# A reciprocal as a power on GpSimd, a second bank, a swapped decoding step and new ranks in an attention and mixture kernel

## The chip, the cores and the metric

One core of a Trainium2 chip. The metric is the device time of one execution, in microseconds (us). The kernel before ran three times: 2363.28, 2365.78 and 2366.66 us; the median is 2365.78 us.

## The reference

Three layers follow one another, on 4 x 576 = 2304 tokens of width 512 (8 heads of 64):

```python
scores = scale * np.matmul(q, k.transpose(0, 1, 3, 2))
kth = np.partition(scores, -top_k, axis=-1)[..., -top_k:-top_k + 1]      # top_k = 32
scores = np.where(scores >= kth, scores, -1000000000.0)
attn = np.exp(scores - np.max(scores, axis=-1, keepdims=True))
attn = attn / (np.sum(attn, axis=-1, keepdims=True) + 1e-09)
x = np.matmul(attn, v)                        # heads side by side: 2304 x 512
...
h = x @ w_in                                  # 512 -> 2048
x = (h * np.cos(h)) @ w_out                   # 2048 -> 512
...
P = np.exp(logits - logits.max())             # logits = x @ w_gate, 8 experts
for _ in range(8):
    P /= P.sum(1, keepdims=True) + 1e-09
    P /= P.sum(0, keepdims=True) + 1e-09
    P *= N / E
for e in range(E):
    out += P[:, e:e + 1] * (np.maximum(x @ w1[e], 0.0) @ w2[e])
```

`w_in` and `w_out` reach the kernel as 64-bit numbers, which it turns into 32-bit ones itself.

## The kernel before, in words

**How the work is cut.** The first three tiles of 128 tokens (the leading tiles) go through attention and the first MLP ahead of everything else, in plain 32-bit matmuls (`attention_tile`, `moe1_tile_a`, `moe1_tile_b`). Their output (`x2fh`, `x2fl`) lets the expert matmuls of these tiles begin (`fill`), which then run on TensorE beside the attention of the rest (`attention`, `moe1`). Later matmuls split every operand into a high and a low part and take three products (lines 506 to 508; 517, 518 and 521 where the low part comes late). After the rest of the attention come the remaining tiles of the first MLP, the gates, and the experts for all other tokens.

**The leading stage.** For each of the 24 (tile, head) pairs `att_tile` multiplies queries and keys (line 582), copies the scores (588), and finds the 32 largest of each row on VectorE in four rounds (590, 593, 594). GpSimd computes the offset of the exponential (595), ScalarE does a leaky step and the exponential with its sum (596, 597). GpSimd adds 1e-9 to the sum (599), VectorE takes the reciprocal (600), GpSimd multiplies the row by it (601). TensorE transposes the row (606), ScalarE copies it (610), TensorE multiplies by the values (664), ScalarE copies the result (668). The attention of the other tokens goes through the same lines, 120 times more, with 624, 625, 632 and 634 in place of 610 and 664.

Beside it the weights are decoded, 16 blocks of `w_in` and 16 of `w_out`, each 128 x 512 (`decode`, called by `fresh` and `pieces`). A DMA brings the block, VectorE shifts the high word (461), ScalarE scales the low word (462), GpSimd adds 768 to the high word (463) and ScalarE takes the sign of what is above 768 (464); GpSimd adds the shifted word and the low word as integers (465) and multiplies by the sign (466). A second DMA keeps the result for the later MLP.

The first MLP of a leading tile: products with `w_in` (762) into two banks in turn, copies (764), the factor cos(h) in `gate` (724 to 731, on GpSimd, VectorE, ScalarE, VectorE), transposes in groups of four (772) into the banks of `trb` in turn, copies (775), 16 second products with `w_out` accumulated in one bank (785), a copy (787), transposes (792), and the two parts of the output (799, 800).

**What sets the order.** Nothing is issued as it stands in the code. `Plan.add` keeps each instruction with its engine, a cost in ns and what it depends on; `Plan.listed` plays the engines forward in time, and gives each engine, whenever it is free, the ready instruction of lowest priority value. The value is that of the class of work (`PRIORITY`); in the leading stage a number from `ORDER` is added, one for each engine, kind of work and unit (a pair of tile and head, a half of a tile's MLP or its second product, a block). The order so found is the order in which each engine then runs, fixed before the launch. `Plan.settle` goes through it once more with paces (`PACE`, or 1.15 times the cost) and puts filler matmuls (line 1203, into a bank of their own) into TensorE's expected gaps, up to 230 us.

The lines that the change touches or that the steps of the prediction name:

```python
hb, trb = Cycle([ps_y[0], ps_h]), Cycle([ps_y[2], ps_y[1]])     # line 748
...
y = ps_y[3]                                                     # line 783
```

So two transposed groups may stand in two banks, and the second products of all three tiles use the same bank.

Of the kernel before, what the change touches and what calls it, by code (L numbers as in the profile page):

```python
# [10 lines left out]
F32 = mybir.dt.float32  # L11
# [3 lines left out]
AF = mybir.ActivationFunctionType  # L15
ALU = mybir.AluOpType
# [6 lines left out]
HALF_PI = 1.5707963267948966  # L23
# [22 lines left out]

ORDER = {
    ("PE", "first attention"): [
        -4.1, -3.9, -2.2, -3.2, -4.2, -2.1, -3.6, -2.9, -3, -3.3, -2.9, -2.6, -2.4, -3.9, -2.9, -2.9,
        -1.9, -2.9, -4.3, -2.9, -3.2, -1.8, -2.1, -3,  # L50
    ],
    ("PE", "first mlp"): [
        -0.8, -1.8, -1.6, 0, -1.1, -1.1, -0.9, 0, -1.5, -1.2, -1.8, 0,
    ],
    ("PE", "decode"): [
        0.7, 1.2, 1.8, 0.4, -0.8, -0.4, -0.4, -0.3, -1.5, -0.4, -0.1, -0.9, -2.1, 0.2, -1.5, -1.6,
        -0.8, -2.6, -0.3, 0.8, -1.5, -0.4, 0.2, -0.4, -0.4, -0.4, 0.3, 1.9, -0.7, -0.6, -0.4, -0.4,
# [12 lines left out]
    ("DVE", "first attention"): [  # L70
        -1, 0.2, -0.3, 0.2, -0.9, 0.8, -0.1, -0.7, 0.2, -0.2, -0.6, 0.6, 0.3, -1.7, 0.3, 0.7,
        0.7, 1, 1.1, 0.4, 0.2, 1.9, 0.2, -1.6,
    ],
    ("DVE", "first mlp"): [
        0.2, 1.2, 0.6, 0, -0.2, 0.8, 0.4, 0, -0.2, 1.1, -0.9, 0,
    ],
    ("DVE", "decode"): [
        -1.8, -0.6, -1.9, 0, -0.5, -2.3, 0.4, 0, -0.9, -0.3, -1.2, -1.1, -1.4, -0.3, -0.3, -1.2,
        -0.3, -2.5, 0, -0.6, -0.2, -0.3, -1.2, -0.1, -0.8, -0.3, 0.7, 0.3, 0, -0.3, -0.3, -2.2,
    ],  # L80
    ("POOL", "first attention"): [
# [58 lines left out]
class Plan:  # L140
# [15 lines left out]
    def buf(self, pool, shape, dtype, name):  # L156
        return Buf(self, pool, shape, dtype, name)
# [200 lines left out]
def fused_kernel(tc, kq, vv, w_in, w_out, w_gate, w1, w2, out, B=4):  # L358
# [4 lines left out]
    V, A_, G_, T_ = nc.vector, nc.scalar, nc.gpsimd, nc.tensor  # L363
# [23 lines left out]
    add, buf = pl.add, pl.buf  # L387
# [25 lines left out]
    x_d = buf("dram", [128, 4, NT], F32, "x_d")
    lg_d = buf("dram", [16, NT], F32, "lg_d")
# [5 lines left out]
    ps_y = [buf("psum", [128, 512], F32, f"y{i}") for i in range(4)]  # L420
    ps_h = buf("psum", [128, 512], F32, "h")
# [145 lines left out]
    def att_tile(stats, dests, plain=None):  # L567
# [4 lines left out]
        sc, m, wk, ex = sc_r(), m_r(), wk_r(), ex_r()  # L572
# [16 lines left out]
        mc = lambda i, k=1: m.ap[:, i : i + k]  # L589
# [7 lines left out]
        put("ACT", act_ns(S, ap=True) + 93.0, lambda: A_.activation(ex.ap, ex.ap, AF.Exp, scale=-0.125 / TINY, bias=mc(32), accum_out=mc(33)),  # L597
            [ex, (m, 32, 33)], [ex, (m, 33, 34)], func="exp")
        put("POOL", 162, lambda: G_.tensor_scalar(mc(34), mc(33), 1e-9, 1.0, op0=ALU.add, op1=ALU.mult), [(m, 33, 34)], [(m, 34, 35)])
        put("DVE", 75, lambda: V.reciprocal(mc(35), mc(34)), [(m, 34, 35)], [(m, 35, 36)])  # L600
        put("POOL", 724, lambda: G_.tensor_scalar(ex.ap, ex.ap, mc(35), 0.0, op0=ALU.mult, op1=ALU.add), [ex, (m, 35, 36)], [ex])  # L601
        pt = lambda: ps_t.ap.rearrange("p (c t) -> p c t", c=4)
        for c0, c1, p in ((0, 4, 128), (4, 5, 64)):
# [8 lines left out]
            for r0, rn, hd, t0 in dests:  # L612
# [629 lines left out]
```

## Time and profile before

| what | value |
|---|---|
| median of three runs | 2365.78 us |
| the profiled execution's own time | 2365.81 us |
| its span, first to last instruction | 2364.0 us |
| busy: TensorE (PE) | 2331.9 us, 99% |
| busy: weight loads (PEld) | 1932.1 us, 82% |
| busy: VectorE (DVE) | 1815.7 us, 77% |
| busy: ScalarE (ACT) | 1333.3 us, 56% |
| busy: GpSimd (POOL) | 1260.4 us, 53% |
| granted TensorE clock, mean | 0.998 of full |

The span is the time from the first instruction to the last; the execution's own time has 1.8 us more around it. The busy shares are averages over stretches with different limits, and matmuls are pipelined, with ends that are modelled: a busy PE is not a PE at its peak. In a row of the trace, "x" gives the count, "a<-b" the tile written and the tiles read, and "<-" in the last column what ended the idle time of the engine just before.

### The profile page before, as it was taken

The numbers are of one execution on the slowest core, as the hardware profiler recorded it, in microseconds if no ns is written. First come the engines' busy times: TensorE is split into PE (matmuls) and PEld (weight loads), VectorE is DVE, ScalarE is ACT, GpSimd is POOL, SyncE is SP. The second block draws the span as 40 slices with busy tenths as digits, with TensorE's granted clock in tenths as the row PEclk, the third lists the DMA queues.
The fourth block names the chain that finished last, engine by engine and source line by source line (L and its number), as shares of the span: only waits on it lengthen the run. The fifth ranks groups of instructions, "written<-read, shape, count | busy, mean of one in ns | idle before, by whom it ended". The sixth has DMA issues, their size and how long they took to land.

```text
span 2364.0 us, 34301 instructions
## 1 busy us (share of the span) xinstructions
PE 2331.9 (99%) x11487; PEld 1932.1 (82%) x11487; DVE 1815.7 (77%) x3340; ACT 1333.3 (56%) x2688; POOL 1260.4 (53%) x1352
## 2 busy tenths in 40 slices
PE   9999999999899999999999999999999999999999
PEld 7655989898677888888888897888888888888887
DVE  7991999999869999999177796876666666666665
ACT  5884888888787777777477675222232222222221
POOL 6982987888876666665401036433333344444440
PEclk9999999999999999999999999999999999999999
DMA  7661654555333333433443332122222221111101
GB/s 222 204 182 40 188 163 141 171 158 169 118 86 94 120 120 120 120 100 95 126 123 108 117 116 65 41 76 77 85 77 80 77 66 36 36 36 36 36 23 49
DMA packets 152464, 242.28 MB, mean 102 GB/s; under 512 B 14624, under 2 KB 61808, under 8 KB 152288
## 3 DMA queue, kind: packets, MB, share of 16 engines
q1 hardware_dynamic: 152288, 240.10, 33.7%
q8 instruction: 90, 1.47, 0.3%
q14 instruction: 86, 0.70, 0.1%
HBM read 208.18 MB, written 31.87 MB: 102 GB/s over the span
## 4 chain that ended last, share of the span: by engine, by line
PE 83%; DVE 7%; POOL 4%; ACT 2%; DMA 2%; issue 2%; SPq 0%; POOLq 0%; ACTq 0%; DVEq 0%
PE y L506 11%; PE y L508 11%; PE y L507 11%; PE g L506 3%; PE g L508 3%; PE g L507 3%; PE t L606 3%; PE h L508 2%; PE h L506 2%; PE h L507 2%; PE y L517 2%; PE y L518 2%; PE t L632 2%; PE y L521 2%; PE s L578 1%
## 5 line engine op out<-in xcount | busy, mean ns | idle before, releaser
L481 POOL TENSOR_TENSOR wlo<-raw,whi 128x512 fp32r<-128x512 f32 x336 | 443.4, 1325 | 141.6 <-ACT whi L479 110.8
L594 DVE MAX8 m<-wk 128x8 f32<-128x576 f32 x432 | 317.7, 749 | 2.7
L1084 DVE SCALAR_TENSOR_TENSOR acc<-y,P,acc 128x512 f32<-128x512 f32 x308 | 229.3, 748 | 103.5 <-PE y L508 103.2
L479 ACT ACTIVATE whi<-raw 128x512 fp32r<-128x512 f32 x416 | 258.0, 626 | 82.5 <-PE y L508 30.4
L593 DVE MATCH_REPLACE8 wk<-m,wk 128x576 f32<-128x576 f32 x288 | 214.1, 744 | 1.9
L506 PE MATMUL y<-whi,gh 128*128 128x512 f32 x448 | 181.1, 404 | 0.0
L508 PE MATMUL y<-whi,gl 128*128 128x512 f32 x448 | 176.3, 394 | 0.0
L506 PE MATMUL y<-gh,xh 128*128 128x512 f32 x450 | 175.9, 391 | 0.1
L507 PE MATMUL y<-wlo,gh 128*128 128x512 f32 x448 | 175.7, 392 | 0.0
L508 PE MATMUL y<-gh,xl 128*128 128x512 f32 x450 | 175.1, 389 | 0.0
L507 PE MATMUL y<-gl,xh 128*128 128x512 f32 x450 | 175.1, 389 | 0.0
L588 ACT ACTIVATE sc<-s 128x288 f32<-128x288 f32 x288 | 116.6, 405 | 36.2 <-PE s L582 20.6
L606 PE MATMUL t<-ident,ex 128*128 128x128 f32 (+1 forms) x720 | 127.3, 275 | 8.0 <-DVE atl L625 3.4
L596 ACT ACTIVATE ex<-sc,m 128x576 f32<-128x576 f32 x144 | 111.1, 772 | 27.0 <-DVE m L594 25.7
L601 POOL TENSOR_SCALAR ex<-ex,m 128x576 f32<-128x576 f32 x144 | 110.8, 770 | 27.6 <-DVE m L600 24.2
L606 PEld LDWEIGHTS t<-ident,ex 128*128 128x128 f32 (+1 forms) x720 | 84.0, 134 | 49.4 <-issue 10.6
L590 DVE MAX8 m<-sc 128x8 f32<-128x576 f32 x144 | 107.5, 747 | 18.8 <-ACT sc L588 18.7
L624 ACT ACTIVATE ath<-t 64x128 fp32r<-64x128 f32 (+3 forms) x272 | 104.2, 395 | 29.0 <-PE t L606 26.1
L597 ACT ACTIVATE ex<-ex,m 128x576 f32<-128x576 f32 x144 | 111.5, 774 | 6.9 <-POOL m L595 2.3
L593 DVE MATCH_REPLACE8 wk<-m,sc 128x576 f32<-128x576 f32 x144 | 106.9, 743 | 0.1
L506 PEld LDWEIGHTS y<-gh,xh 128*128 128x128 f32 x450 | 84.5, 188 | 18.6 <-DVE acc L1080 0.8
L508 PE MATMUL y<-gh,gl 128*128 128x512 f32 x254 | 99.5, 392 | 0.0
(378 smaller groups left out, 7047.2 us busy)
## 6 DMA issues: line engine op xcount, KB each, us to landing
raw<-in_w_dram SPq DMA_DIRECT2D x384, 256.0 KB, 2.7
kq<-in_kq_dram SPq DMA_DIRECT2D x40, 576.0 KB, 4.0
raw<-win_d SPq DMA_DIRECT2D x64, 256.0 KB, 3.0
raw<-wout_d SPq DMA_DIRECT2D x64, 256.0 KB, 2.7
y_d<-st SPq DMA_DIRECT2D x56, 256.0 KB, 3.0
raw<-y_d SPq DMA_DIRECT2D x56, 256.0 KB, 2.7
d_raw<-in_w_in_dram SPq DMA_DIRECT2D x16, 512.0 KB, 5.4
d_raw<-in_w_out_dram SPq DMA_DIRECT2D x16, 512.0 KB, 3.7
```

Source lines behind the costliest of these rows:

```text
L479: put("ACT", act_ns(n), lambda: A_.activation(hv(), rv(), AF.Copy), [rb], [hb])
L481: put(e, c, lambda: f.tensor_tensor(lv(), rv(), hv().bitcast(F32), op=ALU.subtract), [rb, hb], [lb])
L506: T_.matmul(o(), ah(), bh(), start=start, stop=False)
L507: T_.matmul(o(), ah(), bl(), start=False, stop=False)
L508: T_.matmul(o(), al(), bh(), start=False, stop=stop)
L588: put("ACT", act_ns(288, psum=True), lambda c=c: A_.activation(sc.ap[:, c], o(), AF.Copy), [ps_s], [(sc, c.start, c.stop)])
L593: put("DVE", 669, lambda r=r, src=src: V.match_replace(wk.ap, mc(8 * r, 8), src.ap, LOWEST), [src, (m, 8 * r, 8 * r + 8)], [wk])
L594: put("DVE", 669, lambda r=r: V.max(mc(8 * r + 8, 8), wk.ap), [wk], [(m, 8 * r + 8, 8 * r + 16)])
L596: put("ACT", act_ns(S, ap=True), lambda: A_.activation(ex.ap, sc.ap, AF.Prelu, scale=-1.0, bias=mc(31), alpha=TINY), [sc, (m, 24, 32)], [ex])
L597: put("ACT", act_ns(S, ap=True) + 93.0, lambda: A_.activation(ex.ap, ex.ap, AF.Exp, scale=-0.125 / TINY, bias=mc(32), accum_out=mc(33)), [ ...
L606: T_.transpose(pt()[:p, c - c0, :], ex.ap[:, c * 128 : c * 128 + p], ident.ap)
L1084: put("DVE", 663, lambda y=y, av=av, pcol=pcol: V.scalar_tensor_tensor(av(), y.ap, pcol(), av(), op0=ALU.mult, op1=ALU.add), [y, P, a], [a])
```

## The change

It does four things. The reciprocal of line 600 becomes a power with exponent -1 (a new column of `cols`) on GpSimd, for all 144 rows of work. The low word's step of the decoding (462) goes to GpSimd, and the addition of 768 to the high word (463) goes to ScalarE. The transposes of the first MLP use one bank, `ps_y[2]`, and the middle leading tile's second product takes the bank so freed, `ps_y[1]`, while the first and the last tile's stay in `ps_y[3]`. All numbers of `ORDER` are new (of its 15 lists, three are shown).

```diff
 ORDER = {
     ("PE", "first attention"): [
-        -4.1, -3.9, -2.2, -3.2, -4.2, -2.1, -3.6, -2.9, -3, -3.3, -2.9, -2.6, -2.4, -3.9, -2.9, -2.9,
-        -1.9, -2.9, -4.3, -2.9, -3.2, -1.8, -2.1, -3,
+        -4, -1.7, -2.5, -3, -3, -0.6, -2.9, -2.5, -3.2, -2.5, -2.5, -2.5, -3.1, -1, -2.7, -2.5,
+        -2.5, -1.9, -1.9, -2.8, -1.4, -1.7, -2.8, -2.5,
     ],
     ("PE", "first mlp"): [
-        -0.8, -1.8, -1.6, 0, -1.1, -1.1, -0.9, 0, -1.5, -1.2, -1.8, 0,
+        -0.7, -1.2, -1.2, 0, -1.9, -1.3, -1.2, 0, -1.2, -1.2, -0.6, 0,
     ],
...
     ("DVE", "first mlp"): [
-        0.2, 1.2, 0.6, 0, -0.2, 0.8, 0.4, 0, -0.2, 1.1, -0.9, 0,
+        -0.8, 0.5, 0.5, 0, 0.5, 0.5, 0, 0, 0.7, 0.5, 0.7, 0,
     ],
...
-    cols = buf("cst", [128, 4], F32, "cols")
+    cols = buf("cst", [128, 5], F32, "cols")
...
-    for i, c in enumerate((HALF_PI, 768.0, -768.0, 2.0)):
+    for i, c in enumerate((HALF_PI, 768.0, -768.0, 2.0, -1.0)):
...
-        put("ACT", 613, lambda: A_.activation(lv(), lo(), AF.Identity, bias=cols.ap[:, 3:4], scale=2.0**-51), [raw, cols], [lb])
-        put("POOL", 724, lambda: G_.tensor_scalar(sgn.ap, hi(F32), 1.0, 768.0, op0=ALU.mult, op1=ALU.add), [raw], [sgn])
+        put("POOL", 724, lambda: G_.tensor_scalar(lv(), lo(), 2.0**-51, 2.0, op0=ALU.mult, op1=ALU.add), [raw], [lb])
+        put("ACT", 613, lambda: A_.activation(sgn.ap, hi(F32), AF.Identity, bias=cols.ap[:, 1:2]), [raw, cols], [sgn])
...
-        put("DVE", 75, lambda: V.reciprocal(mc(35), mc(34)), [(m, 34, 35)], [(m, 35, 36)])
+        put("POOL", 250, lambda: G_.tensor_tensor(mc(35), mc(34), cols.ap[:, 4:5], op=ALU.pow), [(m, 34, 35), cols], [(m, 35, 36)])
...
-    hb, trb = Cycle([ps_y[0], ps_h]), Cycle([ps_y[2], ps_y[1]])
+    hb, trb = Cycle([ps_y[0], ps_h]), Cycle([ps_y[2]])
...
-        y = ps_y[3]
+        y = ps_y[3 - 2 * (t % 2)]
```

## Rows read from the trace of the kernel before

PE is TensorE, PEld its weight loads, DVE VectorE, ACT ScalarE, POOL GpSimd.

**Rows 1.** Busy time by stretch: length, then busy us of PE, PEld, DVE, ACT, POOL.
```profile
25.00:175.00 150.00, 146.56 (x736) 88.93 (x734) 141.16 (x283) 123.44 (x251) 131.91 (x159) 1.00 0.63 193
175.00:236.00 61.00, 59.27 (x237) 31.24 (x236) 11.33 (x16) 27.99 (x55) 17.81 (x23) 1.00 0.15 46
236.00:590.00 354.00, 352.92 (x2062) 318.18 (x2062) 344.30 (x777) 295.62 (x698) 298.53 (x366) 1.00 0.55 165
590.00:730.00 140.00, 124.74 (x605) 100.39 (x604) 114.27 (x195) 113.61 (x209) 105.70 (x101) 0.98 0.34 99
730.00:1110.00 380.00, 379.47 (x1989) 316.02 (x1988) 374.00 (x825) 293.24 (x654) 244.89 (x318) 1.00 0.37 112
```

**Rows 2.** The filler of line 1203: PE and PEld busy up to 125 us.
```profile
0.00:125.00 125.00, 48.43 (x304) 42.65 (x305) 1.00 0.71 214
```

**Rows 3.** Timeline of VectorE (start us, us), at 49 us and at 173 us.
```profile
49.55 0.14 DVE L600 RECIPROCAL m<-m 128x1 f32<-128x1 f32 x1
49.61 0.07 DVE L593 MATCH_VALUE_LOAD wk<-m,wk 128x8 f32 x1
...
173.62 0.76 DVE L594 MAX8 m<-wk 128x8 f32<-128x576 f32 x1
```

**Rows 4.** Timeline of GpSimd, the last decoding products.
```profile
171.38 2.52 POOL L466 TENSOR_TENSOR wout_s<-wout_s,raw 128x512 f32<-128x512 f32 x2
```

**Rows 5.** Chain of waits by line, 175 to 236 us, then 590 to 730 us.
```profile
by line: PE y L785 43.1%; PE t L664 9.6%; issue 5.1%; PE y L772 4.9%; ACT whi L479 4.1%; PE t L606 3.9%; DVE rr L731 3.5%; PE h L762 2.8%; POOL kl L481 2.6%; DVE rr L726 2.0%; ACT x2fh L799 1.8%; POOL tt L724 1.7%; ACT rr L727 1.7%; POOL rr
...
by line: DVE rr L731 8.4%; DVE gl L481 7.8%; issue 7.4%; PE y L517 5.3%; PE y L518 5.2%; PE y L521 5.0%; DVE rr L726 3.8%; PE t L632 3.4%; DVE m L594 3.4%; DMA raw<-win_d 3.2%; DVE wk L593 3.1%; POOL wlo L481 2.8%; DMA y_d<-st 2.6%; PE t L6
```

**Rows 6.** What TensorE waited for, 590 to 730 us (us, times, longest).
```profile
PE t L632 <- DVE ath L625: 4.6, 1, 4.6
```

**Rows 7.** VectorE by line, 0 to 236 us: busy, mean ns, idle before.
```profile
L594 DVE MAX8 m<-wk 128x8 f32<-128x576 f32 x72 | 52.4, 745 | 0.2
...
L600 DVE RECIPROCAL m<-m 128x1 f32<-128x1 f32 x24 | 3.6, 148 | 3.8 <-POOL m L599 3.7
```

**Rows 8.** GpSimd by line, 0 to 236 us.
```profile
L463 POOL TENSOR_SCALAR raw<-d_raw 128x512 f32<-128x512 f32 x32 | 23.5, 739 | 10.8 <-DMA d_raw<-in_w_in_dram 8.8 <-DMA d_raw<-in_w_out_dram 1.5
...
L599 POOL TENSOR_SCALAR m<-m 128x1 f32<-128x1 f32 x24 | 6.2, 257 | 8.2 <-ACT ex L597 6.6
...
L562 POOL TENSOR_TENSOR qt<-kq,qt 64x64 fp32r<-64x64 f32 x2 | 0.6, 322 | 0.0
```

**Rows 9.** Timeline of GpSimd, its first operation with two inputs.
```profile
12.16 1.27 POOL L465 TENSOR_TENSOR win_s<-d_mag,win_s 128x512 int32<-128x512 int32 x1 [1.35 <-DVE d_mag L461]
```

**Rows 10.** What GpSimd waited for, 0 to 236 us.
```profile
POOL win_s L465 <- ACT win_s L462: 5.0, 4, 3.2
...
POOL ex L601 <- DVE m L600: 1.9, 5, 0.7
```

**Rows 11.** ScalarE by line, 0 to 236 us.
```profile
L464 ACT ACTIVATE raw<-raw,cols 128x512 f32<-128x512 f32 x32 | 22.8, 716 | 2.7 <-POOL raw L463 2.7
...
L462 ACT ACTIVATE wout_s<-d_raw,cols 128x512 f32<-128x512 uint32 x16 | 12.2, 764 | 2.0 <-DMA d_raw<-in_w_out_dram 2.0
```

**Rows 12.** Timeline of TensorE in the tail of the leading stage.
```profile
210.83 0.66 PE L772 MATMUL y<-ident,rr 128*128 128x128 f32 x4 [0.48 <-DVE rr L731]
212.27 0.66 PE L772 MATMUL y<-ident,rr 128*128 128x128 f32 x4 [0.79 <-DVE rr L731]
...
217.06 1.04 PE L772 MATMUL y<-ident,rr 128*128 128x128 f32 x8
```

**Rows 13.** Timeline of ScalarE, the copy after the first of these groups.
```profile
211.52 0.60 ACT L775 ACTIVATE gT<-y 128x512 f32<-128x512 f32 x1 [1.47 <-PE y L772]
```

**Rows 14.** Line 772 up to 125 us and after.
```profile
0.00:125.00 125.00, 1.04 (x8) 0.94 (x8) 1.00 0.71 214
125.00:236.00 111.00, 5.73 (x40) 4.49 (x40) 1.00 0.34 103
```

**Rows 15.** VectorE by line, 590 to 730 us.
```profile
L600 DVE RECIPROCAL m<-m 128x1 f32<-128x1 f32 x12 | 1.9, 158 | 4.9 <-POOL m L599 4.6
```

**Rows 16.** Line 600 in 236 to 590 us: busy time and count.
```profile
236.00:590.00 354.00, 7.69 (x50) 1.00 0.55 165
```

**Rows 17.** Timeline of TensorE, the first expert's first product.
```profile
235.81 0.39 PE L506 MATMUL g<-x2fh,whi 128*128 128x384 f32 x1
```

More of the change, by code (lines that the diff above doesn't have):

```diff
@@ L54 @@
     ],
     ("PE", "decode"): [
-        0.7, 1.2, 1.8, 0.4, -0.8, -0.4, -0.4, -0.3, -1.5, -0.4, -0.1, -0.9, -2.1, 0.2, -1.5, -1.6,
-        -0.8, -2.6, -0.3, 0.8, -1.5, -0.4, 0.2, -0.4, -0.4, -0.4, 0.3, 1.9, -0.7, -0.6, -0.4, -0.4,
+        -1.9, -0.5, -0.5, -0.5, -1.6, -0.1, 0.3, -0.2, -0.5, 0, -0.5, -0.9, -0.1, -0.5, -0.2, -1,
+        0.8, -0.5, -0.8, 1.1, -0.9, -2.5, 1.3, -0.7, -1.4, -2, -2.3, -0.5, 0.9, -0.2, 0.8, 0.1,
     ],
     ("ACT", "first attention"): [
-        -2.4, -1.3, 0.9, -0.1, -1.2, -1.4, -2.1, -3, -1.2, -2.1, -1, -0.8, -2.6, -0.1, -3.3, -1.8,
@@ L61 @@
-        -1.1, -1, -1.2, -1.7, -1.2, 0.2, -1.2, -1.1,
+        -0.3, -0.7, -0.3, 0.1, -0.8, -1.1, -0.6, 0.8, -0.7, 0.1, 0.1, 0.1, 0.1, 0.1, 0, 0.1,
+        0.1, -0.4, 0.1, -2.1, 0.1, 0.9, 0.1, 0.9,
     ],
     ("ACT", "first mlp"): [
-        0.5, 0.8, -0.7, 0, -0.1, 0.5, 1.1, 0, 0.7, 1, -0.2, 0,
+        -1.2, 0.5, 0.1, 0, 0.5, 1.8, 0.5, 0, 0.8, 2, 0.5, 0,
     ],
     ("ACT", "decode"): [
-        0.5, 2.5, 1.7, 1.2, 1.4, 2, 1.7, 1.7, 2, 2.4, 1.3, 1.6, 1.7, 2.4, 1.6, 2.1,
-        1.1, -0.5, 1.7, 2, 0.3, 1.5, 1.2, 1.9, 1.7, 2.7, 2.1, 0.3, 2.1, 1.7, 2.9, 1.7,
+        3.1, 2.1, 0.5, 2.7, 2, 2.7, 2.7, 2.7, 2.3, 2.4, 1.9, 1.1, 0.5, 1.9, 1.8, 1.9,
@@ L69 @@
+        3.1, 2.3, 1.6, 2.8, 1.5, 2.9, 0.5, 2.1, 2.1, 3.1, 1.2, 1.5, 3, 2.2, 3.3, 1.7,
     ],
     ("DVE", "first attention"): [
-        -1, 0.2, -0.3, 0.2, -0.9, 0.8, -0.1, -0.7, 0.2, -0.2, -0.6, 0.6, 0.3, -1.7, 0.3, 0.7,
-        0.7, 1, 1.1, 0.4, 0.2, 1.9, 0.2, -1.6,
+        1.2, 0.7, -0.9, -1.3, -1.7, -0.8, -1.7, -0.9, -0.8, -1.9, -0.8, 0.7, -1, 0.2, -1.3, 0.6,
+        -2.3, -0.8, -0.7, -2.8, -0.8, 0, -2.8, 0,
     ],
     ("DVE", "first mlp"): [
-        0.2, 1.2, 0.6, 0, -0.2, 0.8, 0.4, 0, -0.2, 1.1, -0.9, 0,
+        -0.8, 0.5, 0.5, 0, 0.5, 0.5, 0, 0, 0.7, 0.5, 0.7, 0,
@@ L76 @@
     ],
     ("DVE", "decode"): [
-        -1.8, -0.6, -1.9, 0, -0.5, -2.3, 0.4, 0, -0.9, -0.3, -1.2, -1.1, -1.4, -0.3, -0.3, -1.2,
-        -0.3, -2.5, 0, -0.6, -0.2, -0.3, -1.2, -0.1, -0.8, -0.3, 0.7, 0.3, 0, -0.3, -0.3, -2.2,
+        -1.6, -2.1, -3.6, -2.8, -3.1, -0.9, -2.3, -2.4, -1.2, -2, -1.7, -2.5, -1.3, -0.5, -1.8, -1.2,
+        0.8, -1.6, -4, -2.4, -2.1, -2.2, -1.7, -1.3, -1, 0.1, -2.5, -2.1, -2.3, -1.4, -1.8, -1.1,
     ],
     ("POOL", "first attention"): [
-        -2.2, -1, 0.3, -0.3, -1, -1.5, -0.1, 1, -1, -1.5, -1, -1.2, -2.1, -3, -1, -2.2,
@@ L83 @@
-        -1, -2.4, -1, -1, -1.3, 0.1, -2.2, -0.7,
+        -1.2, -2.6, -3.4, -2, -2, -1.5, -1.1, -2.3, -0.8, -1.5, -1.5, -1.9, 0.9, -1, -0.5, -1.9,
+        -1.8, -0.6, -1.5, -1.5, -2.7, -0.7, -0.4, -0.2,
     ],
     ("POOL", "first mlp"): [
-        0.4, -0.2, 1.8, 0, -0.2, 1.6, 1.3, 0, 1.7, 1.1, 0.6, 0,
+        -2.4, 0.4, -1.2, 0, -0.3, -0.9, -1, 0, -0.5, -1.2, -0.5, 0,
     ],
     ("POOL", "decode"): [
-        0.9, 0.8, 0.8, 0.7, 2.9, 2, 0, -1.9, 1.9, 1.3, -1.1, 0.7, 3.3, -0.2, 0.8, 2.3,
@@ L90 @@
-        0.2, -1.4, -2.7, 1.4, 0.6, 0.1, -0.3, 1.1, 1, 0.8, -0.1, 2.3, -0.6, 1, 0.8, 0.2,
+        0.5, 2.6, -0.6, 0, -0.8, 1.8, 1.4, 1.1, 1.3, 1.4, 0.9, 0.1, 1.3, 0.9, 0.8, 1.3,
+        0.2, 0.9, -0.1, 1.8, 0.5, 0.9, 1.9, 0.7, 2, 2.1, 0.9, 0.8, 2.6, 1.2, 1.7, 1.5,
     ],
     ("SP", "first attention"): [
-        -1.2, 1.6, 0.4, -0.5, -0.9, 0.4, 0, 0, 0, 2.7, -0.4, -0.7, 0.6, -1, -0.7, 0.9,
-        1.7, -1.1, 0, 1.4, -0.3, -3.2, -1.1, 0.2,
+        -0.8, -0.6, 0.9, -0.8, 0.2, 0.2, -0.1, 0.2, 1, 0.2, -1, -0.6, 0, 0.6, 1.6, 0.7,
@@ L95 @@
+        0.2, 0.2, -1.4, -0.3, 0.7, 1, 1.7, 1,
     ],
     ("SP", "first mlp"): [
-        0.2, -0.5, 0.2, 0, -0.4, -0.7, -0.7, 0, -0.7, 0.6, -1.4, 0,
+        -0.8, -0.3, -1, 0, -1, -0.7, -0.8, 0, 0.2, -0.7, -1.7, 0,
     ],
     ("SP", "decode"): [
-        1, 0.2, -1.2, -0.4, -1.1, 0.7, -1.5, -0.8, -1.6, -1.3, -0.7, -0.2, -1.1, 1, -0.9, -0.8,
-        -1.6, -3, -0.8, -2.9, -1, -0.8, -0.4, -0.4, -1, -1, -1, -2, 0.2, -0.8, -0.7, 0.3,
+        -0.9, -0.9, -0.7, -0.8, 2.9, -1.2, -1.3, 0.8, 0, 0.6, 0.1, -0.5, 0.5, 0, 0, -0.9,
@@ L102 @@
+        -0.2, 0.1, -0.6, -1.2, 1, 0.9, 0.1, -0.1, -1.4, -0.5, -0.7, -1.6, 0.2, 0.4, -0.9, 0.8,
     ],
```

## The prediction

> **What bounds the kernel now.** I first cut the span into stretches and read the busy time of each engine in each [rows 1]. From 236 us on TensorE is the bound: 352.92 of 354 us up to 590, 379.47 of 380 us from 730 to 1110. A microsecond taken from another engine there buys nothing, with one exception: between 590 and 730 us TensorE is busy for 124.74 of 140 us, so 15.3 us are lost. Before 236 us lies the leading stage (three token tiles, decoding of the weights), where TensorE's figure misleads: 48.43 us of its busy time before 125 us are the filler matmuls of line 1203 [rows 2]. Real work is short there because of its suppliers: between 25 and 175 us VectorE is busy for 141.16 of 150 us and GpSimd for 131.91 [rows 1], the two nearly level. VectorE's last top-k step of this stage starts at 173.62 us and GpSimd's last two decoding products at 171.38 us [rows 3, 4]. After that the chain of waits runs on TensorE, 43.1% of 175 to 236 us in the second product of line 785 alone [rows 5]: this tail gets shorter only if more of its matmuls can run before 125 us, in place of filler. In 590 to 730 us the chain has no single owner: VectorE's gate steps, GpSimd, a DMA and TensorE take turns [rows 5], and one TensorE wait, line 632 for VectorE's line 625, costs 4.6 us at a stroke [rows 6].
>
> **Part 1, the reciprocal.** 144 one-column reciprocals leave VectorE, 24 of them in the leading stage, and 144 one-column powers join GpSimd between lines 599 and 601.
> VectorE: an isolated reciprocal starts at 49.55 us and the next instruction at 49.61 us [rows 3], so it occupies its queue for 0.06 us although its record is 148 ns long. 24 x 0.06 = 1.4 us, and the 3.7 us in which VectorE stood before it for line 599 [rows 7] go too: 5.1 us in all. Nothing else is late behind it: the instructions queued there are mostly top-k steps, and those of line 594 wait 0.2 us in all [rows 7].
> GpSimd: no row shows a power. The cheapest one-column operation there is line 599, 257 ns in the mean; the smallest with two tensors is the 64x64 subtraction of line 562, 322 ns [rows 8]; the lowest full-width one is 1.27 us [rows 9]. I take 0.30 us, because a one-column operation is nearest to the first two, and keep 0.26 and 1.27 as ends; below 0.26 it can't be, since it has one input more than line 599. 24 x 0.30 = 7.2 us come on. Line 601 no longer waits for VectorE: 1.9 us go [rows 10].
> What the row says of a first use: the first two-input operation on GpSimd waits 1.35 us for VectorE's result, nothing more, and takes 1.27 us [rows 9]. The Trainium skill (GPSIMD Engine Reference, 2.1 Instruction dispatch) says that the first call of a freshly loaded GpSimd kernel costs about 6 us more, with no instruction to be seen. By the row the first power costs 0.30 us and the sum below stands; by that page it is an estimated 6 us on GpSimd, once.
>
> **Part 2, the low word.** Per decoded block, line 462 moves from ScalarE to GpSimd and line 463 from GpSimd to ScalarE; 32 of each. On GpSimd I price the new one at the 739 ns of the one that leaves [rows 8]: same shape, same stride. The change of the input to unsigned integers is not shown there; on ScalarE it makes 764 against 716 ns [rows 11], so 0 to 1.5 us over 32. ScalarE is as long as before within the same 1.5 us, and it is not tight (123.44 of 150 us [rows 1]). What changes is who waits: GpSimd's line 465 stood 5.0 us for ScalarE's line 462 [rows 10]; now both stand in one queue, and that goes. No DMA is added, and the block's buffer is still released by the same three engines.
> GpSimd's balance: +7.2 - 1.9 - 5.0 = +0.3 us, and 0 to 1.5 for the integers. It stays level, so decoding neither gains nor loses.
>
> **Part 3, the banks.** All transposes of the first MLP now share one bank; the second of a pair must wait until ScalarE has copied the first. In the tail a group of four starts at 210.83 us [rows 12], its copy at 211.52 us, for 0.60 us [rows 13]: 1.29 us from start to free bank, where now eight in a row take 1.04 us, 0.5 us for four [rows 12]. Of the 48 records of line 772, 40, five pairs of six, come after 125 us [rows 14]: 5 x 0.8 = 4.0 us at worst. I take 0, because second-product matmuls are ready to stand between; without that cover it is the 4.0 us. The middle tile's second product gets a bank of its own, so the last tile's need not wait for the copy of it. TensorE's gaps there are 0.48 and 0.79 us [rows 12], and it is full otherwise: 0 to 1.3 us gained; I take 0.
>
> **Part 4, the ranks.** New ranks reorder the queues of the leading stage; their effect is not in the trace. Ends: all 48.43 us of early filler turned into work, or a badly placed instruction, for which the 4.6 us of [rows 6] is the price seen here. I take 0.
>
> **Sum.** Leading stage: VectorE's 5.1 us reach the end only as far as filler becomes work; GpSimd, level with it, does not get faster. Ends 0 and 5.1; I take 3.
> 590 to 730 us: 12 reciprocals, with 4.6 us of waiting for GpSimd before them [rows 15]; with 12 x 0.06 that is 5.3 us on an engine that the chain passes through again and again, though other waits stand right behind (gate steps for ScalarE). Ends 0 and 5.3; I take 3. Besides, 50 reciprocals fall in 236 to 590 us [rows 16]: 3 us by which attention is further along at 590; hidden by TensorE until then, counted in the range alone. From 730 us on: nothing, TensorE covers it.
> The profiled execution took 2365.81 us (span 2364.0 and 1.8 around it), as good as the median of 2365.78. 2365.8 - 3 - 3 = 2359.8, so 2360.
>
> **Rivals.**
> *The order fills the early gaps.* Power and low word need no round trip between engines, so that the queues pack better. For it: 48.43 us of filler, and 18.1 us of GpSimd's 150 idle. Against it: VectorE's sum is nearly a bound, 141.16 of 150 us. If a fifth of the filler becomes work, 9.7 us, with the full 5.3 us later: 2351.
> *Nothing lands.* TensorE's tail starts from the same place because GpSimd, not VectorE, sets the decoding; other waits take over at 590 us. For it: the near-level balance of the two, and the gate's wait for ScalarE behind each stall. Time 2366. A first-use stall belongs here: GpSimd's idle 18.1 us would take in most of one. The 6 us of that page would bring 2360 to at most 2366.
> *Late pieces in a fixed queue.* Every engine runs its list in order; with new ranks one more wait such as line 632's 4.6 us, and the transposes' 4.0 us uncovered: 2374. For it: the wait is there today. Against it: before 590 us TensorE hardly waits.
> *GpSimd becomes the bound.* The power is a slow one. At 1.27 us, 24 make 30.5 us against 18.1 us idle between 25 and 175 us: decoding ends 12.4 us later. In 236 to 590 us 50 make 63.5 us, against 55.5 us idle (298.53 of 354 busy): 8.0 us more, as the low words of the weights come late. 2365.8 + 12.4 + 8.0 = 2386. It decides from 18.1 / 24 = 0.75 us per power on. Against it: no one-column operation comes near that.
>
> **How the numbers follow.** A measurement of this kernel tells about 0.2% from no change, 4.7 us: faster means under 2361.1, slower over 2370.5. Forecast 0.42 (its own range 2355 to 2364, 0.34 of it faster, 0.08 within); order fills gaps 0.18; nothing lands 0.22; late pieces 0.11; GpSimd the bound 0.07. Faster 0.34 + 0.18 = 0.52, same 0.08 + 0.22 = 0.30, slower 0.18. Range: from 2347, where both stretches give their full ends, the 3 us of earlier attention and some of the filler, to 2375, one late piece and uncovered transposes; outside lie the slow power and the edges of two cases, some 0.15.
>
> **What would show it.** Right: no VectorE record at line 600, some 144 GpSimd records there of 0.25 to 0.35 us, no idle before line 601 for VectorE, none at line 465 for ScalarE; the first expert's first product, at 235.81 us now [rows 17], starts at some 233 us; TensorE's loss between 590 and 730 us falls from 15.3 to some 12 us; beyond 730 us the same length. Wrong in size: filler before 125 us changes by more than 5 us. Wrong in kind: GpSimd's powers at 0.75 us or more, GpSimd above 97% busy between 25 and 175 us, or TensorE waiting for ScalarE's copies at line 772 in the tail.

## The result and the profile after

The changed kernel takes 2378.18 us in the median of six runs (2370.01 to 2382.60), the kernel before 2363.91 us on the same chip (2361.38 to 2366.66): a ratio of 1.0059 with a 95% interval of 1.0041 to 1.0078. It is slower, by 0.6%, and lies 3.2 us above the predicted range. The profiled execution took 2378.16 us (span 2376.3), so it stands for the median.

The busy time by stretch, in the columns of [rows 1], for the kernel after:

```profile
25.00:175.00 150.00, 144.38 (x703) 87.73 (x703) 134.44 (x256) 119.33 (x242) 135.52 (x171) 0.97 0.58 180
175.00:236.00 61.00, 57.83 (x219) 29.01 (x218) 13.83 (x20) 32.27 (x58) 26.73 (x32) 1.00 0.21 69
236.00:590.00 354.00, 348.47 (x2036) 312.17 (x2035) 335.65 (x714) 292.71 (x685) 319.00 (x407) 1.00 0.54 162
590.00:730.00 140.00, 126.86 (x621) 103.22 (x620) 124.26 (x199) 116.08 (x215) 121.90 (x119) 0.99 0.35 103
730.00:1110.00 380.00, 375.54 (x1970) 310.84 (x1969) 370.56 (x768) 290.80 (x659) 274.38 (x373) 1.00 0.37 111
```

Read it against [rows 1] for TensorE's idle time: 1.1 becomes 5.5 us from 236 to 590 us, 0.5 becomes 4.5 us from 730 to 1110 us, and only 590 to 730 us improves, from 15.3 to 13.1 us. GpSimd is 20.5 us busier from 236 to 590 us and 29.5 us busier from 730 to 1110 us. The other half of the story is where the first expert begins and when decoding ends. Timelines of TensorE and GpSimd, kernel after:

```profile
238.31 0.39 PE L506 MATMUL g<-x2fh,whi 128*128 128x384 f32 x1
...
189.17 2.49 POOL L466 TENSOR_TENSOR wout_s<-wout_s,raw 128x512 f32<-128x512 f32 x2
```

The first expert product comes 2.5 us later than in [rows 17]. The rest, from there to the end of the span, grew from 2128.2 us (2364.0 - 235.81) to 2138.0 us (2376.3 - 238.31). So 2.5 us were lost in the leading stage and 9.8 us behind it. TensorE's idle time in the three stretches from 236 to 1110 us grew by 6.3 us in all, from 16.9 to 23.1. The remainder, some 3.6 us, is busy time: from the first expert product to the expert stage of all other tokens (at 1454.0 us before, at 1466.4 after) the same number of matmuls within one takes 1202.2 us in place of 1198.6. Why was not followed.

The power itself, from the records of line 600 in the kernel after (least, median and longest in ns, first and last start):

```profile
L600 POOL TENSOR_TENSOR m<-m,cols x144: 548/563/1599, 38.5 to 1118.1; 128x1 f32<-128x1 f32 x144
```

GpSimd by line from 0 to 236 us, kernel after, in the columns of [rows 8]:

```profile
L601 POOL TENSOR_SCALAR ex<-ex,m 128x576 f32<-128x576 f32 x24 | 18.1, 757 | 0.4
...
L600 POOL TENSOR_TENSOR m<-m,cols 128x1 f32<-128x1 f32 x24 | 15.2, 646 | 0.5
...
L462 POOL TENSOR_SCALAR win_s<-d_raw 128x512 f32<-128x512 uint32 x16 | 12.2, 766 | 9.4 <-DMA d_raw<-in_w_in_dram 9.3
...
L599 POOL TENSOR_SCALAR m<-m 128x1 f32<-128x1 f32 x24 | 5.8, 240 | 6.1 <-ACT ex L597 4.2
```

A power on one column takes 563 ns, more than twice line 599, which has the same one column. Of the two waits that the change was to remove, one went: line 601 now stands 0.4 us in all. The other went only in part. Line 465 no longer waits for ScalarE's line 462, but it stands once for 2.9 us where the profile names ScalarE's line 463 (in e12 its longest wait, 2.9 us too, is put down to VectorE's line 461). Its idle time in all falls from 8.4 to 5.2 us:

```profile
POOL win_s L465 <- ACT raw L463: 2.9, 1, 2.9
```

### The profile page after: what moved, and what is told of

Its sections match the earlier page's. It is cut to its first block, busy times and chain, and to the rows that moved or that the text cites. A ratio compares the mean times of both kernels' runs of the same rounds, so it can differ in the third digit from the quotient of the medians.

```text
span 2376.3 us, 34220 instructions
## 1 busy us (share of the span) xinstructions
PE 2334.3 (98%) x11443; PEld 1928.8 (81%) x11443; DVE 1811.4 (76%) x3197; ACT 1335.0 (56%) x2688; POOL 1346.2 (57%) x1496
## 4 chain that ended last, share of the span: by engine, by line
PE 80%; POOL 8%; DVE 6%; ACT 3%; issue 2%; DMA 2%; POOLq 0%; SPq 0%; ACTq 0%; DVEq 0%
PE y L506 11%; PE y L508 11%; PE y L507 11%; PE g L506 3%; PE g L508 3%; PE g L507 3%; PE t L606 3%; PE h L508 2%; PE h L506 2%; PE h L507 2%; PE y L521 2%; PE y L517 1%; PE y L518 1%; PE g L1203 1%; PE t L632 1%
## 5 line engine op out<-in xcount | busy, mean ns | idle before, releaser
L481 POOL TENSOR_TENSOR xl<-raw,xh 128x512 fp32r<-128x512 f32 (+1 forms) x16 | 20.8, 1304 | 142.4 <-ACT xh L479 139.6
L508 PEld LDWEIGHTS y<-whi,gl 128*128 128x128 f32 x448 | 84.1, 188 | 19.3 <-DVE gl L890 0.6
```

The costliest lines, as they stand in the source:

```text
L481: put(e, c, lambda: f.tensor_tensor(lv(), rv(), hv().bitcast(F32), op=ALU.subtract), [rb, hb], [lb])
L508: T_.matmul(o(), al(), bh(), start=False, stop=stop)
```

## The experiments

Fourteen kernels were run. The table gives the median, the ratio to the kernel before on the same chip with its interval, and, from the profile, the start of the first expert product (the lead) and the rest of the span (us).

| kernel | median | ratio | lead | rest |
|---|---|---|---|---|
| before | 2363.91 | 1 | 235.8 | 2128.2 |
| after | 2378.18 | 1.0059 [1.0041, 1.0078] | 238.3 | 2138.0 |
| e1_cheap | 2371.05 | 1.0029 [1.0015, 1.0043] | 237.0 | 2132.1 |
| e2_oldranks | 2378.37 | 1.0059 [1.0042, 1.0077] | 246.7 | 2129.9 |
| e3_power_only | 2382.86 | 1.0081 [1.0062, 1.0099] | 244.3 | 2136.5 |
| e4_recip_dve | 2387.93 | 1.0093 [1.0061, 1.0124] | 256.7 | 2128.1 |
| e5_newranks_only | 2386.09 | 1.0100 [1.0085, 1.0115] | 258.0 | 2125.3 |
| e6_lead_power | 2374.78 | 1.0033 [1.0016, 1.0049] | 241.3 | 2134.3 |
| e8_double | 2423.15 | 1.0245 [1.0224, 1.0266] | 254.0 | 2170.7 |
| e9_lowword_only | 2374.09 | 1.0046 [1.0031, 1.0061] | 252.0 | 2121.1 |
| e10_banks_only | 2366.57 | 1.0019 [1.0007, 1.0030] | 239.3 | 2125.5 |
| e11_none | 2364.82 | 0.9994 [0.9981, 1.0007] | 237.3 | 2128.5 |
| e12_dve_in_slot | 2371.39 | 1.0020 [1.0005, 1.0035] | 233.5 | 2137.3 |
| e13_split | 2361.28 | 0.9990 [0.9981, 1.0000] | 234.6 | 2124.6 |
| e14_lead_only | 2368.29 | 1.0012 [0.9998, 1.0025] | 240.1 | 2126.3 |
| e15_priced | 2373.08 | 1.0039 [1.0025, 1.0054] | 239.8 | 2130.6 |

### The parts by themselves, and why they mislead

The kernel after with the old ranks:

```
-    ("PE", "first attention"): [-4, -1.7, -2.5, ...
+    ("PE", "first attention"): [-4.1, -3.9, -2.2, ...
...
```

> The changed kernel with the ranks of before: power, low word and banks are changed, the 15 lists are the old ones. Theory load: still slow, 2374 to 2382. Theory ranks: 2362 to 2368, as before.

The kernel before with the power alone (fifth constant column included):

```
-        put("DVE", 75, lambda: V.reciprocal(mc(35), mc(34)), ...)
+        put("POOL", 250, lambda: G_.tensor_tensor(mc(35), mc(34), cols.ap[:, 4:5], op=ALU.pow), ...)
```

> The kernel before with the power on GpSimd alone; ranks, low word and banks as before. Theory load: 2372 to 2380, most of the 14 us lost. Theory ranks: 2361 to 2367, no loss.

The kernel after with the reciprocal back on VectorE, planned there:

```
-        put("POOL", 250, lambda: G_.tensor_tensor(mc(35), mc(34), cols.ap[:, 4:5], op=ALU.pow), ...)
+        put("DVE", 75, lambda: V.reciprocal(mc(35), mc(34)), ...)
```

> The changed kernel with the reciprocal back on VectorE; low word, banks and the new ranks stay. Theory load: 2358 to 2366, the loss is gone. Theory ranks: 2374 to 2382, the loss stays, as the ranks are the new ones (which were searched with the power in the place).

Three more are the kernel before with one part of the change: e5 takes the new numbers of ORDER alone, e9 the two lines of the low word, e10 the banks:

```
e9  -        put("ACT", 613, lambda: A_.activation(lv(), lo(), AF.Identity, ...
e9  -        put("POOL", 724, lambda: G_.tensor_scalar(sgn.ap, hi(F32), ...
e9  +        put("POOL", 724, lambda: G_.tensor_scalar(lv(), lo(), 2.0**-51, 2.0, ...
e9  +        put("ACT", 613, lambda: A_.activation(sgn.ap, hi(F32), AF.Identity, ...
```

> The kernel before with the new ranks alone; reciprocal on VectorE, low word and banks as before. Theory that ranks fit one plan only: the leading stage ends 10 to 30 us later, 2372 to 2395, with 2128 us behind it. Rival, that the new ranks are simply better or worse ones: 2358 to 2368.

> The kernel before with the low word's step on GpSimd and the addition of 768 on ScalarE; nothing else. Theory that ranks fit one plan only: any change of the plan under the old ranks lengthens the leading stage by 5 us or more, 2368 to 2385, with 2128 us behind the first expert's first product. Rival, that this step is harmless or helps: 2360 to 2366.

> The kernel before with one bank for the transposes and the middle tile's second product in a bank of its own; nothing else. Theory that ranks fit one plan only: 2366 to 2385, all of it ahead of the first expert's first product. Rival, that the banks are harmless: 2360 to 2366.

All six are slower than before, and all six have a longer lead: 239.3 to 258.0 us in place of 235.8. With the new ranks, undoing the power made the kernel slower still (e4, where 2358 to 2366 was expected); with the old ranks the banks, the low word and the power lose too. e2 and e5 came out in a range that was named, e9 too, e10 at the edge of one; e3 lies above both of its ranges. The filler of line 1203 up to 125 us, in the columns of [rows 2], in e5:

```profile
0.00:125.00 125.00, 60.29 (x402) 54.89 (x402) 0.90 0.67 207
```

and in e9:

```profile
0.00:125.00 125.00, 60.01 (x400) 53.15 (x400) 1.00 0.68 208
```

Both hold 60 us of filler where [rows 2] has 48.43: real work has left the early stretch. In e5 no instruction is another than before, only the ranks are, and the lead is 22 us longer: in all six, a set of ranks on a plan that it was not searched for gave a longer lead. So a part that is taken out where the planner sees it is measured together with an order that doesn't fit, and the leads of these runs can't price the parts. Behind the lead no ranks are added; there e3 shows 2136.5 us with the power against 2128.2 without, 8.3 us more. That alone is weak, because the later order still depends on how the lead was planned: the seven kernels of the table that have VectorE's reciprocal planned there differ by up to 7.1 us in the rest (before, e4, e5, e9, e10, e13, e14: 2121.1 to 2128.2 us).

One pair prices the ranks with the rest of the change in place: e2 and the kernel after differ in the ranks alone, and take the same time, 2378.37 and 2378.18 us. The new ranks make the lead 8.4 us shorter (246.7 to 238.3) and the rest 8.1 us longer (2129.9 to 2138.0).

### One order, another operation in the same place

So the next runs keep the plan of the kernel after and all its queues, and change only what is issued in the power's place. In the traces of the kernel after and of these five every engine has the same instructions in the same order, line 600 and the fillers left out. e1 issues a multiply-add that writes a constant, e6 keeps the power in the 24 places of the leading stage and puts that multiply-add in the 120 others, e8 issues the power twice, e11 nothing (line 599 writes the constant itself), e12 the reciprocal on VectorE. In e1, e6 and e11 a constant takes the place of the reciprocal of the sums, everywhere or in those 120 places.

```
e1   +  lambda: G_.tensor_scalar(mc(35), mc(34), 0.0, 0.03125, op0=ALU.mult, op1=ALU.add)
e8   +  lambda: [G_.tensor_tensor(..., op=ALU.pow), G_.tensor_tensor(..., op=ALU.pow)]
e11  +  lambda: None
e12  +  lambda: V.reciprocal(mc(35), mc(34))
```

> The changed kernel with the power replaced by a one-column multiply and add that gives the constant 1/32; the planner's numbers are untouched, so every engine runs the same order. The reciprocal of the sums is left out, the rows are scaled by 1/32 instead. Theory load (each power takes 0.56 us of GpSimd where 0.30 was taken, 144 of them, and GpSimd's later pieces come late to TensorE): the operation falls to some 0.2 us, 52 us of GpSimd's time go, and the kernel comes back to 2364, 2360 to 2368. Theory ranks (the new order loses the time, whatever the power takes): 2378, 2374 to 2382.

> The changed kernel's own order; the power stays in the 24 rows of work of the leading stage, and the 120 others get the one-column multiply and add by a constant instead (their rows are scaled by 1/32, the reciprocal is left out there). Theory load in the later attention: as the run with all 144 replaced, 2371, at most 2374; the stretch behind the first expert's first product is 2132 us long instead of 2138. Theory that the leading stage carries it: 2376 to 2380.

> The changed kernel's own order with every power done twice on GpSimd: 144 x 0.56 = 81 us more there. Theory load: 52 us less of GpSimd's time bought 7 us, and GpSimd is 90% busy from 236 to 590 us, so 81 us more cost at least 11 us: 2389 or more, up to 2420. Rival, the order alone: 2376 to 2384.

> The changed kernel's own order without any instruction in the power's place: line 599 writes the constant 1/32 and line 601 multiplies by it, so the reciprocal and the sum's addition are left out, and GpSimd has 144 instructions less. Theory load: another 28 us of GpSimd's time go, 2364 to 2369, and the stretch behind the first expert's first product takes 2128 to 2131 us. Rival, that the new order itself costs what is left: 2369 to 2373, no better than with the cheap operation.

> The changed kernel's order, but the operation in the power's place is VectorE's reciprocal, put into VectorE's queue where the plan has the power; all other queues as in the changed kernel, and the result is the reference's. Theory load: GpSimd is relieved of 81 us and VectorE gets 144 waits for line 599: 2364 to 2371. Rival, that waits in VectorE's queue cost as much as the powers on GpSimd: 2376 or more.

GpSimd's time in that place over 144 calls, by the medians of the records, against the time of the kernel: none, 2364.82 us; 27.6 us (0.192 each), 2371.05; 81 us (0.563 each), 2378.18; twice that, 2423.15. The time follows what this one small operation costs on GpSimd, with everything else the same, and steepens: 13.4 us for the first power, 45 us for the second. Of the expectations, e11's was met by its theory of load; e1 and e6 fell between their two ranges, e8 came out above its range, and e12 just above the upper end of its theory of load.

TensorE's idle time from 236 to 1110 us goes the same way: 16.4 us with nothing in the place (e11), 18.3 with the multiply-add (e1), 23.1 with the power, 46.4 with two. The three stretches of e11, in the columns of [rows 1]:

```profile
236.00:590.00 354.00, 352.36 (x2076) 319.38 (x2074) 343.01 (x733) 299.03 (x702) 300.25 (x367) 1.00 0.56 165
590.00:730.00 140.00, 129.18 (x628) 104.10 (x627) 124.55 (x200) 117.66 (x219) 114.56 (x109) 0.98 0.35 100
730.00:1110.00 380.00, 376.10 (x1967) 311.64 (x1966) 365.36 (x757) 288.45 (x652) 243.12 (x316) 1.00 0.38 112
```

Against the kernel after, 3.9 us of idle time are gone between 236 and 590 us and 2.3 us between 590 and 730. From 730 us on it is different: e11 is idle for 3.9 us there, with nothing in the place, and the kernel after for 4.5. The loss against [rows 1] in that last stretch belongs to the later order, not to the time that the powers take. What TensorE waits for shows by which way in e8 (236 to 1110 us: total, times, longest):

```profile
PE s L579 <- POOL kl L481: 10.5, 10, 2.7
PE s L578 <- ACT sc L588: 10.2, 13, 2.1
```

Line 481 makes on GpSimd what rounding leaves over of keys and weights: it stands in one queue with the powers, and TensorE waits for it. In the kernel after the same two waits have grown from 0.3 and 0.7 us before to 2.8 and 4.5 us. What TensorE waits for in the kernel after, from 236 to 1110 us:

```profile
PE t L606 <- DVE x L640: 5.1, 2, 4.2
PE t L606 <- DVE ath L625: 4.7, 5, 1.4
PE s L578 <- ACT sc L588: 4.5, 8, 1.0
PE s L579 <- POOL kl L481: 2.8, 5, 0.9
```

and in e11, where line 579 has no wait for line 481:

```profile
PE t L606 <- DVE x L640: 5.5, 2, 4.1
PE s L578 <- ACT sc L588: 2.9, 4, 1.3
...
PE t L606 <- DVE ath L625: 2.5, 3, 1.3
```

So the longest wait, of line 606 for line 640, and more than half of line 578's come with the order. Line 579's wait is the one that only the powers bring.

In the lead, a constant distance shows that the end of GpSimd's decoding sets where TensorE's tail ends. GpSimd's last decoding products and the first expert product in e8:

```profile
204.84 2.50 POOL L466 TENSOR_TENSOR wout_s<-wout_s,raw 128x512 f32<-128x512 f32 x2
...
254.02 0.39 PE L506 MATMUL g<-x2fh,whi 128*128 128x384 f32 x1
```

254.02 - 204.84 = 49.18 us; in the kernel after 238.31 - 189.17 = 49.14. In e1, e6, e12, e13, e14 and e15 it is 49.15 to 49.20, whether decoding ends early or late; before it was 235.81 - 171.38 = 64.43. (e11's last product stands by itself in the trace; counted from the end of that product the distance is 46.61 us in e11 and 46.65 in the kernel after.) In the new order TensorE's tail behind decoding is 15 us shorter. GpSimd time that is added counts there in full: from one power to two, 24 x 0.563 = 13.5 us were added, and decoding ended and the experts began 15.7 us later. Time that is taken away counts for less: with the multiply-add (e1) GpSimd has 8.9 us less to do and decoding ends 1.4 us earlier, with nothing (e11) 13.5 us less and 1.0 us earlier, with the reciprocal on VectorE (e12) 13.5 us less and 4.8 us earlier. GpSimd's idle time from 25 to 175 us shows where it goes: 14.5 us in the kernel after, 24.2 in e11.

e12 has the best lead, 233.5 us, and a rest that is as long as after's: there the reciprocals stand in VectorE's queue at places that were planned for GpSimd, and line 601 waits for them 66 times, for 50.6 us in the whole run (40 times, 24.2 us, before). So an operation in the wrong place of another queue can cost as much as the power on GpSimd. e11 is the odd one, and e1 with it. With nothing at all in the place its lead should be the shortest, and is 237.3 us. Why it is not stays open.

### Each stage's powers, with everything else held

The deciding pair keeps the order of the kernel after in the leading stage, and lets the 120 later reciprocals be planned on VectorE. e13 issues the 24 early ones on VectorE from the power's place, e14 as the power; nothing else differs, and the traces show the same instructions in the same order on every engine.

```
e13  +  put(*(("POOL", 250) if plain else ("DVE", 75)), lambda: V.reciprocal(mc(35), mc(34)), ...)
e14  +  put(*(("POOL", 250) if plain else ("DVE", 75)),
e14  +      lambda: G_.tensor_tensor(..., op=ALU.pow) if plain else V.reciprocal(mc(35), mc(34)), ...)
```

> The changed kernel with VectorE's reciprocal everywhere: in the leading stage put into VectorE's queue where the plan has the power (the leading stage's order stays that of the new ranks), in the later attention planned on VectorE as before. Theory load: the leading stage ends as in the run with all reciprocals in such places (first product of the first expert near 233.5 us), the rest takes 2128 us as before: span 2362, time 2361 to 2366, level with before or 1 to 3 us below it. Rival, that low word, banks and ranks cost something by themselves: 2368 or more.

> The run e13_split with powers on GpSimd in the 24 rows of work of the leading stage; TensorE's queue is the same in every instruction, the later attention keeps VectorE's reciprocals. 24 x 0.56 = 13.4 us more for GpSimd between 25 and 190 us. If the leading powers carry a good part of the loss: 2366 to 2371, with the first expert's first product 3 to 7 us later than in e13_split (234.6 us). If nearly all of it is in the later attention: 2360 to 2364.

The last decoding products and the first expert product, in e13:

```profile
185.40 2.58 POOL L466 TENSOR_TENSOR wout_s<-wout_s,raw 128x512 f32<-128x512 f32 x2
...
234.60 0.39 PE L506 MATMUL g<-x2fh,whi 128*128 128x384 f32 x1
```

and in e14:

```profile
190.96 2.49 POOL L466 TENSOR_TENSOR wout_s<-wout_s,raw 128x512 f32<-128x512 f32 x2
...
240.12 0.40 PE L506 MATMUL g<-x2fh,whi 128*128 128x384 f32 x1
```

What TensorE waits for in e14, from 175 to 250 us:

```profile
PE y L785 <- POOL wout_s L466: 1.3, 1, 1.3
```

The times of both lie in the range of their theory of load. Decoding ends 5.6 us later with the 24 powers and the first expert product comes 5.5 us later; the wait of line 785 for line 466 is in e14, and in that stretch of the kernel after too, and not in e13. The rest of the span differs by 1.7 us. The lead of one order scatters, though: the kernels with the power there (after, e6, e14, e15) have 238.3 to 241.3 us, those with the VectorE reciprocal (e12, e13) 233.5 and 234.6. The means, 239.9 and 234.1 us, differ by 5.8. The clock is not the reason: in the profiles of the kernel after, e12 and e15 the granted clock is down to half (1.2 GHz) between about 9 and 33 us, in those of e6, e13 and e14 it is full there, and the difference is 5.5 us among the first three and 6.1 among the others. One of e14's ten runs took 2359.23 us, as short as e13's; no profile shows such a run.

The last run is the kernel after with the later powers planned at what they take:

```
-        put("POOL", 250, lambda: ...
+        put("POOL", 250 if plain else 560, lambda: ...
```

> The changed kernel with the later 120 powers planned at 560 ns instead of 250; the leading stage's order and all instructions stay, the later order follows the new price. Theory wrong price: the plan then leaves room for them, and the later loss goes: 2364 to 2370. Theory load: a plan that knows the price can't make room on a GpSimd that is 90% busy, 2373 to 2382, as the changed kernel.

The time, 2373.08 us, lies in the range that was named for the load, not in that for the price. But TensorE's cover returns, with GpSimd as busy as in the kernel after. Three stretches of e15, in the columns of [rows 1]:

```profile
236.00:590.00 354.00, 351.05 (x2058) 315.27 (x2058) 336.73 (x716) 294.69 (x690) 320.75 (x409) 1.00 0.55 163
590.00:730.00 140.00, 126.59 (x619) 103.73 (x618) 112.36 (x183) 112.68 (x208) 114.22 (x112) 0.98 0.36 103
730.00:1110.00 380.00, 379.58 (x1985) 315.22 (x1984) 374.88 (x776) 293.52 (x663) 279.74 (x380) 1.00 0.38 112
```

and of e13, without powers:

```profile
236.00:590.00 354.00, 352.52 (x2068) 318.28 (x2067) 345.69 (x781) 296.49 (x699) 299.42 (x367) 1.00 0.54 165
590.00:730.00 140.00, 125.73 (x611) 101.36 (x610) 115.40 (x197) 114.40 (x209) 105.58 (x102) 0.98 0.34 100
730.00:1110.00 380.00, 379.77 (x1990) 316.21 (x1989) 374.62 (x827) 293.14 (x656) 245.63 (x319) 1.00 0.37 113
```

From 730 us on TensorE is idle for 0.4 us in e15, as in e13 (0.2), and for 4.5 us in the kernel after. The one thing that differs from the kernel after is the price in the plan, and through it the later order. From 236 to 590 us 2.95 us are idle, against 1.5 in e13 and 5.5 after. Over the three stretches it is 16.8 us in e15 and 16.0 in e13, against 23.1 in the kernel after and 16.4 in e11. So the order planned at 250 ns costs TensorE little idle time as long as nothing is issued in the place, and 6.8 us more with the powers; an order planned at 560 ns takes the same powers without it. That 250 ns always plans badly is not shown: e2 was planned at 250 ns too, on the old ranks, and is idle for 0.8 us from 730 to 1110 us.

The steps from e13 to the kernel after, in medians: 2361.28 (e13), + 7.0 for 24 powers in the lead (e14), + 4.8 for 120 powers later, planned at their real price (e15), + 5.1 for the later order that the plan's 250 ns gives, = 2378.18. They add up by themselves, since each is the difference of two neighbours; what they tell is the size of each. How the time is lost behind the lead is followed for about half of it: from e13 to the kernel after the rest grows by 13.4 us, 7.1 of them idle time of TensorE, and most of the others are busy time of the same matmuls (1195.6, 1200.7 and 1202.2 us in e13, e15 and after, counted as in the section on the result), for a reason that stays open. By the ratios, which take out the chip's drift between jobs, the steps are 0.0022, 0.0027 and 0.0020, or 5.2, 6.4 and 4.7 us; each is uncertain by 4 to 6 us, their sum, 0.0069 or 16.3 us, by 5. The sum is clear of the noise; that the last step alone is over nothing rests on TensorE's idle time, not on the time of the runs.

e13 is also the only version with the reference's result that may be ahead of both kernels: 1.75 us under the kernel before, with an interval that touches no change, and 17 us under the kernel after. With the reciprocals on VectorE, the other three parts are together worth 0 to 4.5 us.

## Why the prediction was wrong

**Part 1, the size of the power, failed.** "I take 0.30 us, because a one-column operation is nearest to the first two": it measured 0.563 us, within the ends kept (0.26 to 1.27), so that 24 bring 13.5 us instead of 7.2. The 5.0 us of line 465's wait were taken off in full and came to 3.2 (8.4 us of idle time before that line became 5.2). GpSimd's balance of +0.3 becomes 13.5 - 1.9 - 3.2 = +8.4 us. In the pair that tests the powers they put off the end of decoding by 5.6 us, the rest of the 13.5 going into waits; "neither gains nor loses" is out. Nor did VectorE's relief, the first 3 us taken off in the sum, reach the end: its last top-k step of the stage starts at 178.58 us, where [rows 3] has 173.62, and the first expert product comes 2.5 us later. The nearest rows by shape were the wrong neighbours: e1's multiply-add in the same place takes 0.192 us, so neither the column nor the place is dear; the power is. (It has two inputs and the multiply-add one. The nearest row with two inputs is line 562, 322 ns on 64 columns [rows 8]; another operation with two inputs on one column was not run.)

**The threshold of the rival "GpSimd becomes the bound" failed too.** It was to decide "from 18.1 / 24 = 0.75 us per power on", as if GpSimd's idle 18.1 us were room. They are not: GpSimd's list is executed in order, and its gaps are waits (between 25 and 175 us after the change, 4.2 us for ScalarE before line 599 and 4.1 us for VectorE before line 595), in which no later power can run. In the kernel after GpSimd is still idle for 14.5 of 150 us, and yet the end of its decoding sets the end of TensorE's tail. The mechanism of that rival, chance 0.07, is a part of what happened, at a lower price per power: the powers put off decoding (5.6 us in place of 12.4) and made GpSimd late for TensorE from 236 to 590 us (3.9 us more idle time than in e11, in place of 8.0). The rest of the 14.3 us is not in it. And decoding ended 17.8 us later than before, of which 14.0 us are there without a power too (e13, 185.40 us): that comes with the new order, which has the shorter tail in return.

**"From 730 us on: nothing, TensorE covers it", and the same of 236 to 590 us, failed.** The cover was read from TensorE's busy time, 352.92 and 379.47 us [rows 1], and that shows only that nobody was late, not by how much. 4.4 us are lost up to 590 us and 4.0 from 730 us on, and the two have different causes. Up to 590 us most of it goes when the powers go (5.5 us of idle time after, 1.6 in e11): they stand in one queue with line 481, and TensorE waits for that. From 730 us on 3.9 us stay without any power (e11), and 0.4 are left under another plan (e15): there it is the later order. The prediction has no term for a change of the order behind the leading stage, and gives no reason for leaving it out. It had the plan's price for the power, 250 ns, before it in the diff and did not weigh it against its own upper end.

**Part 4, ranks at nothing, was right in number by luck.** With the rest of the change in place, old and new ranks take the same time (e2, 2378.37 us, and after, 2378.18), because 8.4 us of shorter lead and 8.1 us of longer rest cancel; nothing in the prediction has either. On a plan that isn't theirs the new ranks cost 22 us of lead (e5). With their own they come with a shorter tail, 49.2 us behind decoding in place of 64.4, and with later decoding. The rival "the order fills the early gaps" is out: the filler fell only from 48.43 to 45.27 us. "Late pieces in a fixed queue" may hold in part: of e11's 3.9 us from 730 us on, 2.7 are line 578 waiting for ScalarE's line 588, in an order that is fixed. One more wait of 4.6 us and the uncovered transposes, which made up its sum, are not there; line 606's 4.2 us stand in place of line 632's 4.6.

**What held.** VectorE has no line 600 and line 601 no wait for it. The low word costs 763 to 766 ns per block on GpSimd in the mean, for the 739 assumed and the 1.5 us allowed over 32. The banks cost little: in the tail TensorE's matmuls of line 772 wait 0.2 us for ScalarE's copies and its weight loads 1.7 us, a wait that they did not have before and that the prediction named as a sign of being wrong, so most of the 4.0 us were indeed covered. The waits after the change, from 125 to 236 us:

```profile
PE y L772 <- ACT gT L775: 0.2, 1, 0.2
PEld y L772 <- ACT gT L775: 1.7, 3, 0.7
```

The loss between 590 and 730 us fell to 13.1 us for the "some 12" predicted, but not for the reason given: e15, with no VectorE reciprocal either, keeps a 4.5 us wait of line 632 and has 13.4 us, and e12, with all reciprocals on VectorE, has 12.2. The stall of a first use did not come. In GpSimd's timeline after:

```profile
38.26 0.19 POOL L599 TENSOR_SCALAR m<-m 128x1 f32<-128x1 f32 x1 [2.76 <-ACT ex L597]
38.54 1.15 POOL L600 TENSOR_TENSOR m<-m,cols 128x1 f32<-128x1 f32 x2
```

The first two powers follow 0.09 us behind line 599 and take 1.15 us together, the price of any two. The Trainium skill (GPSIMD Engine Reference, 2.1 Instruction dispatch) gives some 6 us for the first call of a freshly loaded kernel; no run here shows it.

## What to carry to other kernels

An operation that the trace doesn't show should be priced at both ends in every place that it enters, the planner's table too: here the power, and the order planned for it at half its price, turned a kernel that is level with the one before into one that is 14 us slower. The idle time of an engine that executes a fixed list is not room for more work; ask which of its waits the new instruction can hide in, and how soon somebody waits for what stands behind it. Where an order was searched for one plan, a part is measured with the queues held and only the instruction exchanged, since a part taken out of the plan measures a broken order. Even then, look whether a loss stays when nothing is issued in the place: what stays belongs to the order.

## What the runs showed of the hardware

A power of one column takes GpSimd 0.563 us, three times the 0.192 us of a multiply-add of one column, with one input, in the same place of the same queue, while the reciprocal that it replaces held VectorE's queue for 0.06 us [rows 3]. A few records of either are far longer (1599 and 1230 ns at most). The time of one kernel also scatters more in some versions than in others, for a reason that stays open: e1 ran between 2362.45 and 2376.75 us in ten runs, e13, with the same early order, between 2358.83 and 2363.93.
